# Capped attention and a spatial gating layer on one core: head pairs in twos, tails merged, and a list scheduler in the source

## The chip, the cores and the metric

One core of one Trainium2 chip runs the whole program. The metric is device time in microseconds (us) of one execution; the number for the kernel before is the median of 3 runs. The engines have short names in the profile: PE is TensorE's matmul pipe (PEld its weight loads), DVE is VectorE, ACT is ScalarE, POOL is GpSimd, SP is the engine whose queue issues all DMAs here. "L213" is line 213 of the kernel's source.

## What is computed

```python
def _attn_ref(q, k, v, cap):                 # (4, 12, 448, 64) each
    scores = np.matmul(q, k.transpose(0, 1, 3, 2)) / np.sqrt(64)
    scores = cap * np.tanh(scores / cap)
    attn = np.exp(scores - np.max(scores, axis=-1, keepdims=True))
    attn = attn / (np.sum(attn, axis=-1, keepdims=True) + 1e-09)
    return np.matmul(attn, v)

def _moe_ref(x, w_in, g_ln, w_sg, b_sg, w_out):   # x (4, 448, 768)
    h = gelu_tanh(x @ w_in)                       # w_in (768, 1024)
    u, v = h[..., :512], h[..., 512:]
    v_n = (v - mean(v)) / sqrt(var(v) + 1e-06) * g_ln
    v_s = np.einsum('ts,bsd->btd', w_sg, v_n) + b_sg[None, :, None]
    return x + (u * v_s) @ w_out                  # w_out (512, 768)
```

x is the attention output with the 12 heads side by side. w_in and w_out arrive as 64-bit words and are decoded to 32-bit floats on the chip.

## The kernel before, in words

**Attention.** The 12 heads of a batch are 6 pairs; a pair's two heads lie on the two halves of the 128 partitions. The 448 keys are cut into three chunks of 128 and a tail of 64, so a pair is 4 units and the program has 96 units (the loop over `g`). For a unit of 128 keys, `scores` makes the scores of both heads (three passes, since q and k are each split into a rounded part and a rest, `hl`; 6 matmuls, L213). For the tail, both heads' 64 keys are put side by side in `kt`, a zero-padded tile that ACT fills by two small copies for each pair (L173), and three full matmuls follow (L199); the first pair's tail is made from the unsplit data (L205). `soft` and `soft2` are tanh (L226) and exp (L229) on ACT: 128x896 for a chunk, 128x448 for a tail. `av` multiplies by the values into `pav` (L242, two matmuls for a unit, one for each head); ACT moves a finished `pav` out (L250). The softmax sums go to `den` by matmuls with a matrix of ones (L261), two units at a time. In batches 1 to 3 DVE first adds the pair's chunks and its tail to one tile (`presum`, L298: two adds of 128x896 and two of 64x448 for each pair). `recip` turns the sums of a batch into reciprocals (L318 to L323).

**The gating layer** of a batch: `norm` scales the six pairs by a matmul of the reciprocals with a selector (L335) and splits the result (L339 to L346); `hv` is the half of w_in that is normalised (four tiles, L373), `hu` the other half (four, L417), `vsg` the product with w_sg (four, L431), `outp` that with w_out (six, L460). Each product is three passes, each with its own weight load. gelu and the normalisation run on ACT and DVE.

**Weights.** `decode` takes 36 chunks of w_in and w_out, 128x256 each: a DMA into one of three pieces of `xu`, or into a free `raw` tile; the low bits (L565 on DVE for the first chunks, L568 on ACT later); L570, L572 and L575 on DVE; an add on POOL (L578); a rounding cast on DVE (L156) or ACT (L158); a subtraction on POOL (L584). The four pieces of w_sg are split by ACT and POOL (L550, L551).

**What orders the work.** The loop over `g` writes the attention in a fixed pattern. Between two units `filler` draws matmuls of the gating layer from a generator, 11 a unit (`RATE`) or 24 while a batch ends (`RATE_OUT`); `wstep` paces the decoding by the unit's number. Work that must lag is put off by `later` and `tick`. The framework then places instructions by program order and the priorities given with `tc.high_priority()`. Every engine runs its own list in order. PSUM: two double banks for scores, one bank for `pav`, one for `den`, two for the gating layer (`ps_g`).

Of the kernel before, what the change touches and what calls it, by code (L numbers as in the profile page):

```python
# [54 lines left out]
def kernel(  # L55
# [4 lines left out]
    vp: bass.AP,  # L60
    cap: bass.AP,
# [18 lines left out]
    NPAIR = B * NP  # L80
    NSTEP = NPAIR * NC
    SPB = NP * NC

    wp = ctx.enter_context(tc.tile_pool(name="wp", bufs=1))
    qk_p = ctx.enter_context(tc.tile_pool(name="qk", bufs=2))
    v_p = ctx.enter_context(tc.tile_pool(name="v", bufs=2))
    sm_p = ctx.enter_context(tc.tile_pool(name="sm", bufs=3))
    raw_s = Slots(wp, NRAW, [128, 2 * S], FP32, "raw")
    xu = wp.tile([128, 2 * NP, S], FP32, name="xu")
    xu_free = list(range(2 * NP))  # L90
    r_s = Slots(wp, 19, [128, 512], FP32R, "r")
    u_s = Slots(wp, 4, [128, S], FP32, "u")
    t_s = Slots(wp, 3, [128, 512], FP32, "t")
    ps_s = ctx.enter_context(tc.tile_pool(name="ps_s", bufs=2, space=PSUM))
    ps_a = ctx.enter_context(tc.tile_pool(name="ps_a", bufs=1, space=PSUM))
    ps_d = ctx.enter_context(tc.tile_pool(name="ps_d", bufs=1, space=PSUM))
    ps_g = ctx.enter_context(tc.tile_pool(name="ps_g", bufs=2, space=PSUM))

    win = [wp.tile([128, KD, DFF], FP32R, name=f"win{s}") for s in range(2)]
    wout = [wp.tile([128, KF, DM], FP32R, name=f"wout{s}") for s in range(2)]  # L100
    wsg = [wp.tile([128, NC, S], FP32R, name=f"wsg{s}") for s in range(2)]
    sel_r = wp.tile([128, NP, 128], FP32R, name="sel_r")
    rds = wp.tile([128, S], FP32R, name="rds")
    ones_sb = wp.tile([128, 3, NP + 31], FP32, name="ones_sb")
# [6 lines left out]
    kt = wp.tile([128, 2, 2 * TL], FP32R, name="kt")  # L111
# [4 lines left out]
    dq = []  # L116
    now = [0]

    def later(d, fn):
        dq.append((now[0] + d, len(dq), fn))  # L120

    def tick():
        now[0] += 1
        while True:
            due = [e for e in dq if e[0] <= now[0]]
            if not due:
                return
            for e in due:
                dq.remove(e)
            for e in due:  # L130
                e[2]()

    def two(t):
        return t.rearrange("p (a s) -> p a s", a=2)

    raws, qks, vs = {}, {}, {}

    def load_pair(P):
        if P >= NPAIR:
            return  # L140
        b, p = divmod(P, NP)
        raws[P] = raw_s.get()
        for i, src in enumerate((q2, k2)):
            nc.sync.dma_start(out=two(raws[P])[:, i], in_=src[b, p])

    def load_v(P):
        if P >= NPAIR:
            return
        b, p = divmod(P, NP)
        t = v_p.tile([128, S + TL], FP32, tag="v", name="v")  # L150
        nc.sync.dma_start(out=t, in_=vp[b, p])
# [8 lines left out]
    def prep_a(P):  # L160
        if P >= NPAIR:
            return
        qks[P] = qk_p.tile([128, 2, 2, S], FP32R, tag="hl", name="hl")
        cast(P // NP in DVE_Q, qks[P][:, 0], two(raws[P]))

    def prep_b(P):
        if P >= NPAIR:
            return
        hl = qks[P]
        nc.vector.tensor_tensor(out=hl[:, 1], in0=two(raws[P]), in1=f32(hl[:, 0]), op=ALU.subtract)  # L170
        for h in range(2):
            rows = slice(64 * h, 64 * h + 64)
            nc.scalar.activation(  # L173
                out=kt[rows, :, TL * h:TL * h + TL], in_=f32(hl)[rows, :, 1, 128 * FC:], func=ACTF.Copy)
        raw_s.put(raws.pop(P))

    def prep_first():
        r = two(raws[0])
        hl = qk_p.tile([128, 2, 2, S], FP32R, tag="hl", name="hl")
        for i in range(2):  # L180
            nc.vector.tensor_copy(out=hl[:, 0, i], in_=r[:, i])
            nc.vector.tensor_tensor(out=hl[:, 1, i], in0=r[:, i], in1=f32(hl[:, 0, i]), op=ALU.subtract)
        qks[0] = hl
        raw_s.put(raws.pop(0))

    sc_t, p_t, s_t, pav_t, xu_t = {}, {}, {}, {}, {}
    den_t, units_in = {}, {}

    def unit(g):
        P, c = divmod(g, NC)  # L190
        return P, c if P == 0 or c > 1 else 1 - c

# [594 lines left out]
```

## Time and profile before

| | |
|---|---|
| time, median of 3 runs | 455.83 us (455.79 to 456.27) |
| the profiled execution | 453.91 us, of which the span of its trace is 452.1 |
| busy in the span | PE 423.3 us (94%), DVE 311.6 (69%), ACT 292.2 (65%), POOL 81.7 (18%) |
| mean granted clock of TensorE | 0.985 of full speed |
| moved from and to HBM | 34.2 MB, 76 GB/s on the mean |

A busy PE is not a PE at its peak: the record of a matmul covers also the time in which it stands behind another one. The time of a stage is therefore read from the starts of the rows in it, and what an engine does in a stage from the view of stretches.

### The profile page before, as it was taken

To read this page: it belongs to the slowest core of one execution; us is meant where nothing else is said; L and a number is where in the kernel's file an instruction comes from. 1 tells how busy PE (TensorE), PEld (TensorE's weight loads), DVE (VectorE), ACT (ScalarE), POOL (GpSimd) and SP (SyncE) were. 2 spreads that over 40 slices of the span, in tenths; PEclk is the share of its full clock that TensorE was granted. 3 is DMA by queue.
4 is the path that set the end of the run, shared out by engine and by line. 5 is a ranking of instruction groups with operands and counts; after the bars stand their busy time and mean duration, and the time that the engine had idled before them with its cause. 6 is when DMAs were issued, how large, how long until landed. Compare 5 with 4: busy or idle time off the path is not lost.

```text
span 452.1 us, 5786 instructions
## 1 busy us (share of the span) xinstructions
PE 423.3 (94%) x2097; PEld 269.7 (60%) x2097; DVE 311.6 (69%) x549; ACT 292.2 (65%) x466; POOL 81.7 (18%) x97
## 2 busy tenths in 40 slices
PE   5998798996999499999999999999999999899996
PEld 2333233562665367756666667666666666579985
DVE  4945637899999764796766654877675563868652
ACT  3899899958767874486787775476778640224410
POOL 0525553266257240000000000000000000000000
PEclk9999989999999799999999999999999999999999
DMA  7673234222424223211202103210101001100012
GB/s 244 220 242 135 91 120 152 70 76 81 134 62 124 85 65 104 83 65 43 63 23 65 41 25 104 82 66 25 40 24 25 0 1 61 61 1 1 1 41 81
DMA packets 20716, 34.21 MB, mean 76 GB/s; under 512 B 3024, under 2 KB 12880, under 8 KB 20688
## 3 DMA queue, kind: packets, MB, share of 16 engines
q1 hardware_dynamic: 20688, 33.85, 23.3%
q8 instruction: 16, 0.26, 0.3%
q14 instruction: 12, 0.10, 0.1%
HBM read 28.34 MB, written 5.51 MB: 75 GB/s over the span
## 4 chain that ended last, share of the span: by engine, by line
PE 73%; DVE 12%; DMA 6%; ACT 5%; POOL 2%; issue 1%; SPq 0%; DVEq 0%; ACTq 0%
PE gp L417 14%; PE gp L460 14%; PE pav L242 12%; PE gp L373 12%; PE sc L213 8%; PE gp L431 8%; DMA xu<-in_w_in_dram 4%; PE sc L199 2%; PE den L261 2%; DVE xu L575 2%; ACT raw L226 2%; DVE raw L298 2%; PE gp L335 1%; ACT raw L229 1%; POOL xu L578 1%
## 5 line engine op out<-in xcount | busy, mean ns | idle before, releaser
L226 ACT ACTIVATE raw<-sc,qsc 128x896 f32<-128x896 f32 (+1 forms) x96 | 86.8, 909 | 39.1 <-PE sc L199 21.4
L229 ACT ACTIVATE raw<-raw,cap_sb 128x896 f32<-128x896 f32 (+1 forms) x96 | 90.0, 943 | 0.7
L242 PE MATMUL pav<-raw,v 128*64 128x448 f32 x384 | 88.8, 565 | 1.6 <-ACT xu L250 1.6
L213 PE MATMUL sc<-hl 64*128 64x448 f32 x432 | 67.5, 413 | 7.7 <-ACT raw L226 7.7
L373 PE MATMUL gp<-win,r 128*128 128x512 f32 x264 | 65.5, 398 | 2.7 <-DVE t L362 2.2
L298 DVE TENSOR_TENSOR raw<-raw,raw 64x448 f32<-64x448 f32 (+1 forms) x72 | 63.7, 885 | 5.0 <-PE pav L242 3.7
L417 PE MATMUL gp<-r,win 128*128 128x448 f32 x288 | 64.5, 372 | 0.0
L460 PE MATMUL gp<-r,wout 128*128 128x448 f32 x288 | 63.1, 371 | 0.0
L213 PEld LDWEIGHTS sc<-hl 64*128 64x128 f32 x432 | 37.4, 192 | 39.7 <-issue 15.5
L417 PEld LDWEIGHTS gp<-r,win 128*128 128x128 f32 x288 | 52.8, 188 | 13.8 <-issue 9.6
L373 PEld LDWEIGHTS gp<-win,r 128*128 128x128 f32 x264 | 48.2, 188 | 20.6 <-issue 6.1
L460 PEld LDWEIGHTS gp<-r,wout 128*128 128x128 f32 x288 | 53.1, 188 | 10.8 <-issue 3.8
L387 POOL TENSOR_TENSOR rs<-rs,pw 128x1 f32<-128x1 f32 (+1 forms) x16 | 9.9, 616 | 254.1 <-DVE rs L386 254.1
L242 PEld LDWEIGHTS pav<-raw,v 128*64 128x64 f32 x384 | 24.5, 139 | 50.6 <-issue 39.6
L431 PE MATMUL gp<-wsg,r 128*128 128x448 f32 x176 | 41.5, 382 | 4.7 <-DVE u L362 4.7
L431 PEld LDWEIGHTS gp<-wsg,r 128*128 128x128 f32 x176 | 33.0, 193 | 14.0 <-issue 5.9
L170 DVE TENSOR_TENSOR hl<-raw,hl 128x896 fp32r<-128x896 f32 x23 | 25.0, 1086 | 9.6 <-ACT hl L158 9.6
L465 DVE TENSOR_TENSOR xu<-xu,gp 128x448 f32<-128x448 f32 x24 | 14.6, 611 | 23.2 <-PE gp L460 23.0
L361 ACT ACTIVATE t<-t 128x448 f32<-128x448 f32 (+2 forms) x32 | 19.3, 602 | 15.6 <-DVE t L356 15.5
L356 DVE SCALAR_TENSOR_TENSOR t<-t,gp 128x448 f32<-128x448 f32 (+1 forms) x28 | 18.0, 644 | 15.8 <-ACT t L355 15.7
L578 POOL TENSOR_TENSOR xu<-xu 128x256 int32<-128x256 int32 x22 | 20.7, 943 | 40.6 <-DVE xu L575 40.6
L261 PE MATMUL den<-raw,ones_sb 128*32 128x448 f32 x168 | 24.6, 570 | 2.1 <-DVE raw L298 2.1
(77 smaller groups left out, 434.6 us busy)
## 6 DMA issues: line engine op xcount, KB each, us to landing
v<-in_vp_dram SPq DMA_DIRECT2D x24, 256.0 KB, 3.1
raw<-in_q_dram SPq DMA_DIRECT2D x24, 224.0 KB, 2.6
raw<-in_k_dram SPq DMA_DIRECT2D x24, 224.0 KB, 3.0
xu<-in_w_in_dram SPq DMA_DIRECT2D x21, 256.0 KB, 2.7
out_dram<-xu SPq DMA_DIRECT2D x24, 224.0 KB, 1.9
raw<-in_w_out_dram SPq DMA_DIRECT2D x11, 256.0 KB, 2.7
u<-in_w_sgT_dram SPq DMA_DIRECT2D x4, 224.0 KB, 7.2
raw<-in_w_in_dram SPq DMA_DIRECT2D x3, 256.0 KB, 2.9
```

What stands on the lines that cost most here:

```text
L170: nc.vector.tensor_tensor(out=hl[:, 1], in0=two(raws[P]), in1=f32(hl[:, 0]), op=ALU.subtract)
L213: nc.tensor.matmul(out=sc[:, h, :S], lhsT=hl[rows, w, 1, 128 * c - 128:128 * c], rhs=hl[rows, m, 0], start=(i == 0), stop=(i == 2))
L226: nc.scalar.activation(out=prob(g), in_=src, func=ACTF.Tanh, scale=qsc)
L229: nc.scalar.activation(out=prob(g), in_=prob(g), func=ACTF.Exp, scale=cap_sb)
L242: nc.tensor.matmul(out=pav_t[P][64 * h:64 * h + 64, :S], lhsT=w, rhs=two(p_t[g])[:, h if c else 0, :], start=(g % NC == 0), stop=(c == NC ...
L261: nc.tensor.matmul(out=t[32 * j:32 * j + 32, :S], lhsT=ones_sb[:, 0 if c else 1 + h, NP - 1 - P % NP:NP + 31 - P % NP], rhs=two(src)[:, h ...
L298: eng.tensor_tensor(out=a, in0=a, in1=w, op=ALU.add)
L373: yield 1, lambda i=i, c=c, a=a, w=w: nc.tensor.matmul(out=ps, lhsT=a[c][:, t * 128:t * 128 + 128], rhs=win[w][:, c, HF:], start=(i == 0), ...
L417: yield 1, lambda a=a, w=w, c=c, st=st, sp=sp: nc.tensor.matmul(out=ps, lhsT=win[w][:, c, f * 128:(f + 1) * 128], rhs=a[c][:, :S], start=s ...
L431: yield 1, lambda i=i, c=c, a=a, w=w: nc.tensor.matmul(out=ps, lhsT=a[c][:, f * 128:(f + 1) * 128], rhs=wsg[w][:, c, :], start=(i == 0), s ...
L460: yield 1, lambda ps=ps, c=c, a=a, w=w, f=f, st=st, sp=sp: nc.tensor.matmul(out=ps, lhsT=wout[w][:, f, c * 128:(c + 1) * 128], rhs=a[f][:, ...
L578: nc.gpsimd.tensor_tensor(out=a, in0=a, in1=hi_w, op=ALU.add)
```

## The change

Three things change together.

1. **Two head pairs make a group of seven units** instead of eight: three chunks of the first pair, one unit that holds the 64-key tails of both pairs, three chunks of the second. The merged tail's scores are four matmuls of 64x64 on the four quarters of the array, straight from the unsplit data (L537), for both pairs; its tanh and exp are 128x896; its values are four matmuls on the quarters (L558), with a tile `vt` of its own DMA. `kt`, its two copies for each pair, and the tail's adds on DVE are gone; the tail goes to `den` as a unit of its own, so a batch of 1 to 3 has 9 units of sums instead of 6.
2. **A list scheduler, `Plan`, is in the source.** Every operation is entered with its engine, an assumed cost, a key, a mode of the array (S scores, A values, D sums, Q quarters, G the rest) and the tiles it reads and writes. `run` repeatedly takes, over all engines, the operation that can start first; of those that can start within 0.04 us of each other on an engine the smallest key goes first, and on PE an operation of another mode has 3.92 added to its key. The order that comes out is emitted as it is (`tc.manual_schedule()`). `filler`, `wstep`, `later` and the fixed pattern are gone.
3. **Tiles and engines.** The three decoding pieces (`xb`) are the only ones, and become room for attention outputs one after the other when 12, 1 and 0 chunks are still to be placed. Four `raw` tiles hold q and k, seven `p` tiles the probabilities. `pav` and the gating layer share three PSUM banks (the gating layer at most two; norm's are not limited); at the end the scores' banks join them. The low bits of the first 12 chunks (4 in the trace of before) and 25 of the 36 casts (10) are on DVE, and so is batch 0's move of `pav` (it was ACT's). The load of `cap` is the first DMA.

```diff
-            for h in range(2):
-                rows = slice(64 * h, 64 * h + 64)
-                nc.tensor.matmul(
-                    out=sc[rows, 0, :S], lhsT=r[rows, 1, 128 * FC:], rhs=r[rows, 0],
-                    start=True, stop=True, skip_group_check=True)
...
-            add(b, 3, [(two(s_t[P])[TL * h:TL * h + TL, h, :], pr) for h, pr in enumerate(heads(small, 0))])
...
-        n = RATE_OUT if boost[0] else RATE
...
+RAWS, PS, RS, US, TS = 4, 7, 19, 4, 3
+G_CAP = 2
+DVE_CAST = (0, 1)
+DVE_EVAC = (0,)
+LOW_DVE = 12
+HI_DVE = 25
+SUMS = (False, True, True, True)
...
+class Plan:
...
+    def run(self):
...
+                first = min(x[0] for x in ests) + 0.04
+                pick = min(
+                    (x for x in ests if x[0] <= first),
+                    key=lambda x: (x[1].key + (SWITCH if e == "pe" and x[1].mode != mode else 0.0), x[1].num))
+                if best is None or pick[0] < best[0]:
+                    best = pick
...
+    sc_p = Pool([pp.tile([128, 2, 512], FP32, name=f"sc{i}") for i in range(2)])
+    ps_p = Pool([pp.tile([128, 512], FP32, name=f"ps{i}") for i in range(3)], {"g": G_CAP})
+    den_p = Pool([pp.tile([128, 512], FP32, name="den")])
...
+        def freed(b):
+            if len(st_p.queues[None]) <= (12, 1, 0)[order.index(id(b.t))]:
+                i = order.index(id(b.t))
+                for s in range(2):
+                    x_p.add(b.end, xb[i][:, s])
+                return True
+            return False
...
+        low = "dve" if j < LOW_DVE else "act"
...
+        big = "dve" if j < HI_DVE else "act"
...
+                def tail():
+                    for s in range(2):
+                        for h in range(2):
+                            rows = slice(64 * h, 64 * h + 64)
+                            nc.tensor.matmul(
+                                out=sc.t[64 * s:64 * s + 64, h, :S], lhsT=raw[s].t[rows, 1, 128 * FC:],
+                                rhs=raw[s].t[rows, 0], start=True, stop=True, skip_group_check=True)
...
+                def tail():
+                    for s in range(2):
+                        rows = slice(64 * s, 64 * s + 64)
+                        for h in range(2):
+                            nc.tensor.matmul(
+                                out=pav[s].t[64 * h:64 * h + 64, :S], lhsT=vtail.t[rows, 64 * h:64 * h + 64],
+                                rhs=p.t[rows, h, :], start=(s == 1), stop=(s == 0), skip_group_check=True)
...
+            units = [(0, c) for c in range(1, FC + 1)] + [(0, 0)] + [(1, c) for c in range(1, FC + 1)]
...
+                if not SUMS[b]:
+                    den_unit(pairs[s], 0 if c else 1, p, akey(i) + DEN, last)
+                elif c == 0:
+                    den_unit(pairs[0], 1, p, akey(i) + DEN)
...
+    with tc.manual_schedule():
+        plan.run()
```

How the instructions stand, at three places. First PE at the start of batch 0; before (`sc` scores, `pav` values, `den` sums, `raw` the probabilities, `xN` how many in a row):

```order
L205 MATMUL sc<-raw_67 64x448 x2
L213 MATMUL sc<-hl 128x448 x18
L242 MATMUL pav<-raw_69,v 64x448 x2
L242 MATMUL pav<-raw_70,v 64x448
L213 MATMUL sc<-hl 128x448 x6
L242 MATMUL pav<-raw_70,v 64x448
L199 MATMUL sc<-hl,kt 128x448 x3
L261 MATMUL den<-raw_69,ones_sb 32x448 x2
```

and with the change, where `ps` are the three shared banks, `p` the probabilities, and L537 and L558 the quarters:

```order
L529 MATMUL sc_133<-hl_89 128x448 x6
L529 MATMUL sc_134<-hl_89 128x448 x6
L529 MATMUL sc_133<-hl_89 128x448 x6
L537 MATMUL sc_134<-raw_85 64x448 x2
L537 MATMUL sc_134<-raw_86 64x448 x2
L548 MATMUL ps_135<-p_96,v_91 64x448 x2
L548 MATMUL ps_135<-p_97,v_91 64x448 x2
L529 MATMUL sc_133<-hl_90 128x448 x6
L529 MATMUL sc_134<-hl_90 128x448 x6
L548 MATMUL ps_135<-p_98,v_91 64x448 x2
L558 MATMUL ps_135<-p_99,vt_94 64x448 x2
L558 MATMUL ps_136<-p_99,vt_94 64x448 x2
```

The tail moved behind the first pair's three chunks, and operations of one kind stand together. Over the whole program the kind of work on PE changes 226 times before and 175 times with the change.

Second, DVE where batch 0's attention ends and its reciprocals are made; before (L298 adds for batch 1, L570 to L575 decoding, L339 norm):

```order
L170 TENSOR_TENSOR hl<-raw_68,hl 128x896
L572 TENSOR_SCALAR raw_72<-raw_72 128x256
L319 SCALAR_TENSOR_TENSOR t_102<-t_102,guard,den 64x448
L298 TENSOR_TENSOR raw_77<-raw_77,raw_67 64x448
L321 RECIPROCAL t_102<-t_102 64x448
L298 TENSOR_TENSOR raw_77<-raw_77,raw_67 64x448
L322 CAST rds<-t_102 64x448
L570 TENSOR_SCALAR xu<-xu 128x256
L323 TENSOR_TENSOR rds<-t_102,rds 64x448
```

and with the change (L388 to L403 and the casts to `win_61` are the decoding, COPY is the move of a finished `pav`):

```order
L312 COPY xa_80<-ps_136 128x448
L312 CAST win_61<-xb_82 128x256
L620 SCALAR_TENSOR_TENSOR t_126<-t_126,guard,den 64x448
L623 RECIPROCAL t_126<-t_126 64x448
L312 COPY xa_81<-ps_137 128x448
L388 TENSOR_SCALAR xb_83<-xb_83 128x256
L394 TENSOR_SCALAR xb_83<-xb_83 128x256
L403 SCALAR_TENSOR_TENSOR xb_83<-xb_83 128x256
L398 TENSOR_SCALAR xb_83<-xb_83 128x256
L624 CAST rds<-t_126 64x448
```

Ahead of the reciprocal 12 chunks were cast to `win` before and 6 are now; the other 30 now stand behind it, between the work of the gating layer.

Third, PE in batch 0's gating layer, where `hu` (L741) goes over to `vsg` (L758); with the change (before, one unit of scores or two of values stood between 11 matmuls of `gp` each time):

```order
L558 MATMUL ps_137<-p_99,vt_94 64x448 x2
L558 MATMUL ps_136<-p_99,vt_94 64x448 x2
L548 MATMUL ps_136<-p_101,v_91 64x448 x2
L548 MATMUL ps_136<-p_102,v_91 64x448 x2
L741 MATMUL ps_135<-r_113,win_61 128x448
L741 MATMUL ps_135<-r_114,win_61 128x448
L741 MATMUL ps_135<-r_113,win_62 128x448
L529 MATMUL sc_133<-hl_89 128x448 x6
L529 MATMUL sc_134<-hl_89 128x448 x6
L548 MATMUL ps_136<-p_98,v_91 64x448 x2
L472 MATMUL den<-p_99,ones_sb 32x448 x2
L472 MATMUL den<-p_101,ones_sb 32x448 x2
```

Two of the three shared banks (136 and 137) are values' here at the same time, and the gating layer has the third, 135; all four tiles of this batch's `vsg` follow in that one bank.

## Rows read from the trace of the kernel before

**Rows 1.** Stretches: start:end, length, busy (xcount) by engine, PEclk, DMA share, GB/s

```profile
0.00:76.70 76.70, 64.41 (x359) 25.44 (x360) 45.11 (x99) 63.91 (x102) 33.30 (x40) 0.98 0.54 175
76.70:200.20 123.50, 112.62 (x537) 70.51 (x537) 103.59 (x181) 88.56 (x155) 41.89 (x45) 0.96 0.29 88
200.20:448.50 248.30, 246.28 (x1206) 173.71 (x1204) 162.26 (x271) 139.68 (x211) 6.56 (x12) 1.00 0.12 39
100.00:140.00 40.00, 35.64 (x174) 22.19 (x173) 38.84 (x73) 30.59 (x56) 21.01 (x23) 1.00 0.30 89
```

**Rows 2.** Chain that ended last: start, length, what

```profile
21.85 4.85 DMA xu<-in_w_in_dram
...
50.79 2.62 DMA xu<-in_w_in_dram
...
76.75 2.86 DVE t L321
...
200.21 2.94 PE gp L373 x12
```

**Rows 3.** ACT's first instruction, from its groups in 0:76.7: xcount, busy, mean ns, idle before

```profile
L226 ACT ACT_TABLE_LOAD x1 | 1.3, 1283 | 6.8 <-DVE guard L661 6.8
```

**Rows 4.** Timeline of ACT, batch 0: start, length, instructions

```profile
11.78 1.91 ACT L226 ACTIVATE raw<-sc,qsc 128x896 f32<-128x896 f32 x2
13.58 1.97 ACT L229 ACTIVATE raw<-raw,cap_sb 128x896 f32<-128x896 f32 x2
```

**Rows 5.** Timeline of PE: start, length, instructions

```profile
3.97 1.76 PE L205 MATMUL sc<-raw 64*64 64x448 f32 x4 [3.97 <-DMA raw<-in_k_dram]
...
30.80 1.48 PE L213 MATMUL sc<-hl 64*128 64x448 f32 x12
...
230.30 2.49 PE L417 MATMUL gp<-r,win 128*128 128x448 f32 x11
232.72 0.88 PE L213 MATMUL sc<-hl 64*128 64x448 f32 x6
233.53 2.50 PE L417 MATMUL gp<-r,win 128*128 128x448 f32 x11
...
236.77 1.72 PE L242 MATMUL pav<-raw,v 128*64 128x448 f32 x8
238.43 2.50 PE L417 MATMUL gp<-r,win 128*128 128x448 f32 x11
...
252.03 0.96 PE L261 MATMUL den<-raw,ones_sb 128*32 128x448 f32 x8
```

**Rows 6.** Timeline of PE, the last stretch

```profile
396.10 13.89 PE L373 MATMUL gp<-win,r 128*128 128x512 f32 x60 [0.33 <-DVE r L344]
409.82 14.76 PE L417 MATMUL gp<-r,win 128*128 128x448 f32 x72
424.42 9.08 PE L431 MATMUL gp<-wsg,r 128*128 128x448 f32 x44
```

**Rows 7.** DVE's groups of the whole span: xcount, busy, mean ns, idle before

```profile
L298 DVE TENSOR_TENSOR raw<-raw,raw 128x896 f32<-128x896 f32 x36 | 39.6, 1101 | 0.6
L298 DVE TENSOR_TENSOR raw<-raw,raw 64x448 f32<-64x448 f32 x36 | 24.1, 668 | 4.5 <-PE pav L242 3.7
L575 DVE SCALAR_TENSOR_TENSOR xu<-xu 128x256 int32<-128x256 int32 x22 | 13.7, 622 | 0.2
...
L572 DVE TENSOR_SCALAR xu<-xu 128x256 int32<-128x256 int32 x22 | 8.6, 392 | 0.5
...
L156 DVE CAST win<-xu 128x256 fp32r<-128x256 f32 x10 | 2.9, 288 | 3.8 <-POOL xu L578 3.8
...
L565 DVE TENSOR_SCALAR xu<-xu 128x256 int32<-128x256 uint32 x4 | 2.2, 554 | 0.1
```

**Rows 8.** Timeline of DVE: one operation in two lengths

```profile
15.70 0.28 DVE L570 TENSOR_SCALAR xu<-xu 128x256 f32<-128x256 f32 x1
...
18.89 0.84 DVE L570 TENSOR_SCALAR xu<-xu 128x256 f32<-128x256 f32 x1
```

More of the change, by code (lines that the diff above doesn't have):

```diff
@@ L1 @@
+from collections import deque
 from contextlib import ExitStack
@@ new lines, with __init__, add, can @@
+class Pool:
+    def __init__(self, tiles, caps=None):
+        self.free = [(0.0, i, t) for i, t in enumerate(tiles)]
+        self.n = len(tiles)
+        self.queues = {}
+        self.caps = caps or {}
+        self.held = {}
+    def add(self, when, t):
+        self.free.append((when, self.n, t))
+        self.n += 1
+    def can(self, bufs):
+        by = {}
+        for b in bufs:
+            k = by.get(b.cls, 0)
+            q = self.queues[b.cls]
+            if len(q) <= k or q[k] is not b:
+                return None
+            by[b.cls] = k + 1
+            if self.held.get(b.cls, 0) + k + 1 > self.caps.get(b.cls, 99):
+                return None
+        if len(self.free) < len(bufs):
+            return None
+        return sorted(self.free)[len(bufs) - 1][0]
+    def take(self, b):
+        e = min(self.free)
+        self.free.remove(e)
+        self.queues[b.cls].popleft()
+        self.held[b.cls] = self.held.get(b.cls, 0) + 1
+        b.t = e[2]
+    def give(self, b):
+        self.held[b.cls] -= 1
+        if b.on_free is None or not b.on_free(b):
+            self.add(b.end, b.t)
@@ L177, in prep_first @@
[L177 to L191, printed above, removed]
@@ L253, in den @@
-    def den(b, units):
-        if b not in den_t:
-            den_t[b] = ps_d.tile([128, 512], FP32, tag="den", name="den")
-            units_in[b] = 0
-        t = den_t[b]
-        for half, (P, c, src) in enumerate(units):
-            for h in range(2):
-                j = 2 * half + h
-                nc.tensor.matmul(
-                    out=t[32 * j:32 * j + 32, :S],
-                    lhsT=ones_sb[:, 0 if c else 1 + h, NP - 1 - P % NP:NP + 31 - P % NP],
-                    rhs=two(src)[:, h if c else 0, :],
-                    start=(units_in[b] < 2), stop=(units_in[b] >= NP * (NC - ADDS[b]) - 2),
-                    skip_group_check=True)
-            units_in[b] += 1
@@ L710, with c_copy, mms @@
-    tail[0] = 1
-    half[0] = False
-    while flushes:
-        flush()
-    while not fill_done[0]:
-        filler(0)
-        tick()
-    while dq:
-        tick()
-_INS = ["q2", "k2", "vp", "cap", "w_in", "g_ln", "w_sgT", "b_sg", "w_out", "ones", "sel"]
+    def c_copy(eng, n, psum=False):
+        if eng == "dve":
+            return c_tt(n) if psum else c_ts(n)
+        return c_act(n, psum)
+    def mms(n, cols=None):
+        return n * ((cols or S) / 2400.0 + 0.012)
+    k_cap, k_ones, k_bsg, k_g, k_sel, k_pw, k_rds = (Buf() for _ in range(7))
@@ L724 @@
+    weights()
+    for b in range(B):
+        attention(b)
+        if b:
+            gated(b - 1)
+    gated(B - 1)
+    with tc.manual_schedule():
+        plan.run()
+_INS = ["q2", "k2", "vp", "vt", "cap", "w_in", "g_ln", "w_sgT", "b_sg", "w_out", "ones", "sel"]
 def kernel(**inputs):
@@ L750 @@
         w_sgT[:128 * FC].reshape(FC, 128, S).transpose(1, 0, 2), _np.concatenate([tail, tail])[:, None]], axis=1)
[L751 removed]
+    ones = _np.zeros((128, 2, NP + 31), _np.float32)
     ones[:, 0, NP - 1::NP] = 1.0
[L753 to L754 removed]
+    for s in range(2):
+        ones[TL * s:TL * s + TL, 1, NP - 2 + s::NP] = 1.0
     sel = _np.zeros((2, 2, 32, NP, 2, D), _np.float32)
```

1107 lines of the change are left out of this document (554 added, 553 removed).

## Prediction

> **What bounds the kernel now.** I read the stretches first, cut at two events of the chain that ended last: the reciprocal of batch 0 at 76.75, and at 200.21 the first matmul of batch 1's gating layer [rows 2]. That gives three stages [rows 1]. In stage A (0 to 76.7, batch 0's attention) ACT is busy 63.9 us of the 69.9 that are left after its first instruction waited 6.8 for `cap` [rows 3]: ACT is the bound. In stage B (76.7 to 200.2, 123.5 us, batch 0's gating layer beside attention) PE is busy 112.6 and DVE 103.6, and in its densest part DVE is busy 38.84 of 40 us [rows 1]: there DVE is the bound, with the weights' decoding between everything else. In stage C (200.2 to 448.5) PE is busy 246.3 of 248.3. Behind it 3.6 us remain for the last add and its DMA, to the span's 452.1.
>
> A busy PE can be busy badly, so I took prices from starts [rows 5, 6]. Gating matmuls: 72 take 14.60 us (409.82 to 424.42), 0.203 each, and 60 of `hv` take 13.72 (396.10 to 409.82), 0.229 each; with the program's 264 of `hv` and 776 others that makes 217.8. Twelve score matmuls take 1.48 and six 0.88, so a unit is 0.60. Among other kinds a unit takes 0.81 (232.72 to 233.53): entering scores costs 0.21. Eleven gating matmuls take 2.42 (230.30 to 232.72), 2.23 without the entry: 0.19 for entering these. Two units of values take 1.66 (236.77 to 238.43), and four sums together 0.96 less the overlap of 0.07, 0.89; if a unit of values and four sums cost the same, that is 0.77, and 0.12 for entering either.
>
> **The change on PE.** Counted in both orders with these prices. Before: 72 units of scores 43.2, 96 of values 73.9, 21 issues of sums 16.2, 23 tails of three full matmuls 14.0 and the first one 0.8; entries 75 to scores, 73 to the gating layer, 78 to others, 39.0; the gating layer 217.8. Sum 404.9. With the change: scores 43.2; 72 units of values 55.4; 24 sets of quarters, 12 for scores and 12 for values; 26 issues of sums, 20.0 (five more, since the tails are no longer added on DVE and four issues are half empty, taken at full price); entries 41, 49 and 85, 28.1.
>
> The price of four quarters has no row before. The first tail runs two quarters on the diagonal, four records, two for each matmul, in a row 1.76 us long [rows 5], in the program's first moments. Four column strips run side by side in 0.77, two row halves do so in every unit of scores. I take 0.77 for four quarters, 18.5 for all; the other bound is that two rows of quarters follow one another, 37.0; less than nothing off 0.77 has no row for it. Sum 383.0: 21.9 us less work for PE, of which 10.9 are entries.
>
> The Trainium skill (TensorE: Matmul & The Clock Gate, Part 3, Measured speedup vs the span model) has a table in which four tiles side by side give 3.07 times, not four. By that, 24 sets would cost 5.6 us more, an estimate from that page; the row of the four strips shows no such loss.
>
> **Stage A.** ACT's list up to the last exp of batch 0 holds 21 units. Two tanh take 1.80 from start to start, and two exp 1.97 less the same overlap of 0.11 [rows 4], so a unit takes 1.83, 38.4 in all. The table load and guard 1.5 [rows 3], and four copies of w_sg and one of the sums, half as wide, at some 0.54 each, make 42.6. Gone from ACT here are the copies to `kt`, the move of `pav`, low bits and casts of weights. If ACT never waits, it is through at 6.8 + 42.6 = 49.4. `cap` is now the first DMA, which could take some 2 us off the 6.8; I leave that out, since q and k must be split before the first scores. ACT was busy 91% of its part of stage A (63.9 of 69.9); at that, 42.6 take 46.6, and the reciprocal starts at **53.4**. PE's work up to the last sums is 39.8, hidden under it. DMA is busy 54% in stage A [rows 1], and the bytes fall a little (v without its padding), so I cost the 12 new loads of `vt` at nothing. SP's own list runs in order, and loads of chunks wait in it for pieces to come free; that wait is covered as long as stage B has the decoding hidden, which is the rival below. So the price of stage A is 23 us won, bounds 49.4 and 60 (ACT idle for 20%).
>
> **Stage B.** Part of that is paid back at once: of the 36 chunks 30 are now decoded behind the reciprocal, 19 before. DVE's list from the reciprocal to the first split tile of batch 1, against the same stretch before: 11 more chunks at L575's 0.62 and two operations like L572's 0.39, +15.4; 19 casts, +5.5; 6 low bits, +3.3; one more split and cast of a pair and a move of `pav`, +2; one tile of output less, -0.6; 12 adds of 128x896 for 14, and the 14 tail adds gone, -2.2 and -9.4 [rows 7]. Together +14, so 117.6 where it was 103.6. PE's work between the same points is 104.5 (144.3 less 39.8), and ACT had 88.6 here and loses the copies to `kt`, so DVE is the bound. At the 97% of its densest part that is **121 us**; bounds: 110, if PE bounds after all, and 135. The first `hv` of batch 1 then starts at 174.4, 25.8 earlier than before.
>
> **Stage C.** Before, 243.2 us of work took 248.3. With the change 238.7 remain (383.0 less the 144.3 ahead of that point); with the same 2.1% on top **243.7**. DVE had 162.3 us here and ACT 139.7 [rows 1], and both lose work; neither is near. The three shared banks cost nothing as long as attention stands between two tiles of one bank, and where it doesn't (the third place of the order: `vsg` in bank 135 alone), one such refill waits for a DVE operation, under 1 us. Bounds 239 and 251.
>
> **Sum.** 53.4 + 121 + 243.7 + 3.6 = 421.7 of span; the profiled execution has 1.8 outside its span, 423.5; the median stands 0.42% above that execution (455.83 to 453.91): **425 us**, 30.5 less. Its own range is 415 to 437.
>
> **Rivals.**
>
> *The decoding sets the pace.* For: only three pieces turn over chunks, two once 12 are left, without the free `raw` tiles of before; in the chain, four turns of the pieces take 28.9 us (first and last of five loads, 21.85 and 50.79) [rows 2], 7.2 each. At that pace 18 chunks of w_in on three pieces take 43 us, and 12 of w_out on two pieces another 43: 53.4 + 86 = 139, about when PE wants them. If queues stretch a turn to 10 us, the last comes at 53.4 + 60 + 60 = 173, with the last output tiles and the next batch's start still behind it: stage B takes some 140 us, 425 + 19 = **444**. DVE and POOL also stand in each other's way: the same L570 takes 0.28 and 0.84 [rows 8], and 23 more DVE operations on chunks (8 low bits, 15 casts) at 0.56 would add 13, 438. Of this the Trainium skill (SBUF — State Buffer, Who interferes with whom) says that the port which the two share is locked for a whole instruction. The two lengths agree with that. Against it: my prices for stage B are means that already hold such waits.
>
> *Quarters run one row after another:* 18.5 more on PE, two thirds of it where PE is the bound: **438**. Against it stand the scores' row halves.
>
> *Stage B is bound by PE:* DVE's list is shorter than my means make it, 110 for 121, and ACT starts early: **412**.
>
> *The shared banks starve PE: slower.* Two of three banks hold values for a group at a time. A gelu chain is four operations on ACT and DVE before its bank is free, 2.5 us if each takes the 0.62 of L575, the nearest row here; with one bank alone each of a batch's eight such tiles waits that long, and sixteen others for one operation: 30 us for a batch, 90 for the three that run beside attention. From a third of that uncovered it decides: the 30.5 are gone, **456** and more. Against it: in the order only a handful of refills follow their own bank directly.
>
> *It doesn't do what it says:* costs in `Plan` only set an order, and if that order stalls each engine a little everywhere, 7% over all stages, the time is the same.
>
> **Chances.** Forecast 0.62, PE-bound stage B or better 0.12, decoding 0.12, quarters 0.07, the same 0.02, starving banks and stalls beyond 0.05. The range takes in quarters and decoding: 411 to 445. What a measurement of this kernel can tell from no change is about 0.2%; faster 0.93, same 0.02, slower 0.05.
>
> **What would show it.** The first reciprocal near 53 and ACT over 85% busy ahead of it; the first `hv` of batch 1 near 174, with DVE over 93% busy in between; four quarters starting 0.77 to 0.9 before the next kind; stage C at 244 with PE never waiting over 1 us for a bank; PE's granted clock below 1.00 only in stages A and B. The prediction is wrong if the reciprocal comes late because PE or the splits (two `hl` tiles) stall batch 0, if POOL's or SP's list holds chunks back, or if PE's list, fixed against assumed costs, waits in stage C for ACT or DVE.

## The result: 435.8 us for 456.0, and the profile after

The changed kernel takes 435.8 us (median of 4 runs), before takes 456.0 beside it: ratio 0.955, 95% interval 0.953 to 0.957, faster by 4.5%. Forecast were 425 (411 to 445), so the direction and the range held and the likeliest time was 11 us too low. The profiled execution of that comparison was the one of the four that took 1306.51 us (last section); what is shown as "after" is a second trace of the same kernel, e1_same: 435.58 us, ratio 0.9559 (0.9514 to 0.9604), span 433.6.

The busy times by stretch, cut where the prediction cut (the first reciprocal of batch 0, the first `hv` of batch 1) and once more at the first `hu` of batch 0:

```profile
core 0: us, PE busy (x) PEld busy (x) DVE busy (x) ACT busy (x) POOL busy (x), PEclk, DMA share, GB/s
0.00:52.20 52.20, 45.25 (x312) 18.02 (x312) 33.52 (x64) 42.74 (x49) 15.18 (x20) 1.00 0.61 196
52.20:107.30 55.10, 41.40 (x211) 23.58 (x207) 52.85 (x117) 35.92 (x51) 27.82 (x31) 0.93 0.35 113
107.30:188.35 81.05, 73.74 (x369) 48.19 (x370) 61.67 (x115) 48.86 (x82) 32.28 (x34) 0.94 0.31 94
188.35:430.00 241.65, 240.94 (x1258) 170.51 (x1257) 151.46 (x249) 133.96 (x188) 6.57 (x12) 1.00 0.11 38
```

Against [rows 1]: stage A is 24.5 us shorter and ACT is still busy 42.74 of it, stage C 6.5 shorter and PE busy all through. Stage B got 12.5 longer (136.0 for 123.5), where a shortening of 2.5 was forecast. It has two parts of different kind: up to the first `hu` DVE is busy 52.85 of 55.1 us and PE only 41.4; behind it DVE has 19 us to spare and PE is busy 91%, part of it at the lower clock level. The events that cut it, from the timelines of DVE and PE (start, duration):

```profile
52.19 2.94 DVE L623 RECIPROCAL t<-t 64x448 f32<-64x448 f32 x1
```
```profile
107.29 6.67 PE L741 MATMUL ps<-r,win 128*128 128x448 f32 x18 [1.67 <-ACT r L314]
```
```profile
188.18 2.25 PE L694 MATMUL ps<-win,r 128*128 128x512 f32 x9
```

The 18 matmuls at 107.29 take 0.371 us each, where 0.203 is the price at 2.4 GHz [rows 6]. PE was busy for only 2.27 of the 5.29 us ahead of them (102.00 to 107.29), and the granted clock of their first 2.7 us is 0.50, the level of 1.2 GHz:

```profile
107.30:110.00 2.70, 2.70 (x7) 2.44 (x8) 2.60 (x8) 1.11 (x3) 2.37 (x2) 0.50 0.27 97
```

Four quarters, from PE's timeline:

```profile
24.43 0.98 PE L537 MATMUL sc<-raw 64*64 64x448 f32 x8
25.35 0.88 PE L529 MATMUL sc<-hl 64*128 64x448 f32 x6
...
92.23 0.98 PE L537 MATMUL sc<-raw 64*64 64x448 f32 x8
93.03 0.93 PE L558 MATMUL ps<-p,vt 64*64 64x448 f32 x8
93.89 2.48 PE L548 MATMUL ps<-p,v 128*64 128x448 f32 x12
```

A set takes 0.92 from start to start with a change of kind, 0.80 ahead of other quarters and 0.86 ahead of values.

### The profile page after: what moved, and what is told of

Read it like the earlier page. It is cut to its first block, busy times and chain, and to the rows that moved or that the text cites. A ratio compares the mean times of both kernels' runs of the same rounds, so it can differ in the third digit from the quotient of the medians.

```text
span 1304.7 us, 5767 instructions
## 1 busy us (share of the span) xinstructions
PE 1291.6 (99%) x2144; PEld 544.0 (42%) x2144; DVE 298.9 (23%) x542; ACT 266.7 (20%) x367; POOL 76.6 (6%) x96
## 4 chain that ended last, share of the span: by engine, by line
PE 99%; DVE 0%; ACT 0%; DMA 0%; issue 0%; ACTq 0%
PE ps L548 15%; PE ps L694 14%; PE ps L741 14%; PE sc L529 12%; PE ps L780 12%; PE ps L758 7%; PE den L472 6%; PE sc L780 4%; PE sc L537 3%; PE ps L558 3%; PE sc L758 2%; PE sc L694 2%; PE sc L741 2%; PE ps L651 1%; PE sc L548 1%; DMA cap_sb<-in_cap_dram 0%
## 5 line engine op out<-in xcount | busy, mean ns | idle before, releaser
L548 PE MATMUL ps<-p,v 128*64 128x448 f32 x276 | 199.4, 1649 | 0.0
L694 PE MATMUL ps<-win,r 128*128 128x512 f32 x228 | 191.9, 1086 | 0.1
L741 PE MATMUL ps<-r,win 128*128 128x448 f32 x252 | 184.0, 987 | 1.7 <-ACT xb L314 1.4
L529 PE MATMUL sc<-hl 64*128 64x448 f32 x432 | 163.4, 958 | 6.3 <-DVE hl L312 6.3
L780 PE MATMUL ps<-r,wout 128*128 128x448 f32 x216 | 160.6, 985 | 0.0
L591 ACT ACTIVATE p<-sc,qsc 128x896 f32<-128x896 f32 x84 | 84.4, 1006 | 306.7 <-PE sc L529 217.8
L741 PEld LDWEIGHTS ps<-r,win 128*128 128x128 f32 x252 | 103.5, 416 | 92.6 <-issue 86.7
L694 PEld LDWEIGHTS ps<-win,r 128*128 128x128 f32 x228 | 93.7, 415 | 99.3 <-issue 90.6
L780 PEld LDWEIGHTS ps<-r,wout 128*128 128x128 f32 x216 | 87.5, 411 | 82.4 <-issue 78.5
L758 PE MATMUL ps<-wsg,r 128*128 128x448 f32 x132 | 97.3, 977 | 0.8 <-DVE t L764 0.8
L758 PEld LDWEIGHTS ps<-wsg,r 128*128 128x128 f32 x132 | 52.9, 409 | 52.7 <-issue 49.3
```

The costliest lines, as they stand in the source:

```text
L529: nc.tensor.matmul(out=sc.t[:, h, :S], lhsT=hl[s].t[rows, w, 1, 128 * c - 128:128 * c], rhs=hl[s].t[rows, m, 0], start=(k == 0), stop=(k = ...
L548: nc.tensor.matmul(out=pav[s].t[64 * h:64 * h + 64, :S], lhsT=v[s].t[:, 128 * (c - 1) + 64 * h:128 * (c - 1) + 64 * h + 64], rhs=p.t[:, h, ...
L591: op("act", c_act(2 * S, True, True), lambda p=p, sc=sc: nc.scalar.activation(out=p.t, in_=sc.t[:, :, :S], func=ACTF.Tanh, scale=qsc), rd= ...
L694: nc.tensor.matmul(out=ps.t[:, :HF], lhsT=(xl if a else xh)[c].t[:, t * 128:t * 128 + 128], rhs=win[w][:, c, HF:], start=(c == 0 and k == ...
L741: nc.tensor.matmul(out=ps.t[:, :S], lhsT=win[w][:, c, f * 128:(f + 1) * 128], rhs=(xl if a else xh)[c].t[:, :S], start=(c == 0 and k == 0) ...
L758: nc.tensor.matmul(out=ps.t[:, :S], lhsT=(vl if a else vh)[c].t[:, f * 128:(f + 1) * 128], rhs=wsg[w][:, c, :], start=(c == 0 and k == 0), ...
```

## Experiments

The stages of every kernel, cut at the first reciprocal, the first `hv` of batch 1 and the end of PE's last matmul (us; before and after on top). "B up to `hu`" is the part of stage B ahead of the first `hu`:

| run | stage A | stage B | B up to `hu` | stage C | span | ratio to before |
|---|---|---|---|---|---|---|
| before | 76.7 | 123.5 | 40.5 | 248.4 | 452.1 | 1 |
| e1_same | 52.2 | 136.0 | 55.1 | 241.9 | 433.6 | 0.9559 |
| e2_switch0 | 52.6 | 153.5 | 56.1 | 249.4 | 459.1 | 1.0128 |
| e3_quads2 | 53.1 | 137.6 | 54.5 | 245.7 | 439.9 | 0.9687 |
| e4_pairtails | 57.0 | 148.9 | 55.3 | 242.6 | 452.2 | 0.9947 |
| e5_two_ops_out | 51.6 | 134.3 | 44.7 | 241.3 | 430.7 | 0.9486 |
| e6_no_whole | 51.5 | 132.5 | 54.6 | 239.5 | 427.1 | 0.9373 |
| e7_pieces2 | 51.9 | 161.6 | 63.7 | 241.3 | 458.3 | 1.0087 |
| e8_casts_act | 52.6 | 142.2 | 51.9 | 241.3 | 439.7 | 0.9700 |
| e9_x_parked | 52.1 | 146.4 | 57.7 | 236.0 | 438.2 | 0.9618 |
| e10_x_parked_3 | 52.7 | 132.8 | 55.5 | 240.7 | 429.8 | 0.9515 |
| e11_one_op_less | 51.3 | 141.9 | 51.0 | 241.3 | 438.1 | 0.9625 |
| e12_one_op_less_parked_3 | 51.9 | 127.7 | 49.5 | 241.3 | 424.5 | 0.9325 |

**The same kernel, the scheduler's entry cost, the quarters, the merged tails.** e1_same is the changed kernel again.

> The changed kernel once more, for a trace of an execution like the timed ones (435.8 us). The 11 us above the forecast of 425 must stand in one of three places. If quarters run one row after another, a set of four takes 1.5 us and not 0.77, and stages A and B are as forecast. If the decoding sets the pace, the first reciprocal is near 53 and the first hv of batch 1 near 185. If the fixed order stalls PE late, that hv is near 174 and stage C takes 255 us instead of 244.

The reciprocal at 52.19 and the `hv` at 188.18 are the second of these three places.

e2_switch0:

```diff
-SWITCH = 3.92
+SWITCH = 0.0
```

> SWITCH is 0: the scheduler no longer prefers work of the kind that PE is doing. PE changes its kind 256 times instead of 175. If each entry costs what the trace of before says (0.12 to 0.21 us), PE has 14.3 us more to do and the time rises by 10 to 14 us, to 446 to 450. If the entries are covered by something else (weight loads, or PE waiting for ACT and DVE anyway), it rises by less than 3.

461.29 us, 25.7 more, where the entries alone make 14.3 and 446 to 450 was expected. Counted in the two traces, 53 of the 81 entries more lie in stage C, 9.6 us by the prices, and it got 7.5 longer; 21 lie in stage B, 3.8 us by the prices, and it got 17.5 longer, at a mean clock of 0.88. So the price of an entry roughly holds where PE is the bound. What made stage B so much longer isn't shown; the order of all lists changed with this edit.

e3_quads2 issues each set of score quarters twice:

```diff
-                    for s in range(2):
+                    for s in (0, 1, 0, 1):
```

> Each set of four score quarters is issued twice (the second one overwrites the first with the same values): 12 sets more. If four quarters run side by side, 0.77 us each, at most 9 us more on PE, 7 of them outside batch 0: 442 to 445. If the two rows of quarters follow one another, 1.5 us each: 14 to 18 more, 450 to 454.

441.52 us, 5.9 more for 12 sets.

```profile
24.83 1.73 PE L537 MATMUL sc<-raw 64*64 64x448 f32 x16
26.50 0.86 PE L529 MATMUL sc<-hl 64*128 64x448 f32 x6
```

Two sets in a row start at 24.83 and the next kind at 26.50: 1.67, which is twice 0.77 and an entry of 0.12. The quarters run side by side. e4, below, shows it once more: there a set has two quarters, and it takes 0.90 to the next kind, where four take 0.92:

```profile
25.10 0.97 PE L536 MATMUL sc<-raw 64*64 64x448 f32 x4
26.00 0.96 PE L472 MATMUL den<-p,ones_sb 128*32 128x448 f32 x8
```

e4_pairtails keeps the scheduler and the new tiles and engines, and gives each pair a tail of its own (two of the four quarters, tanh and exp of half the width, the tails added to the sums by DVE again):

```diff
-            units = [(0, c) for c in range(1, FC + 1)] + [(0, 0)] + [(1, c) for c in range(1, FC + 1)]
+            units = [(s, c) for s in range(2) for c in (1, 2, 3, 0)]
...
-                    op("pe", mms(4), tail, rd=raw, wr=[sc], key=akey(i), mode="Q")
+                    op("pe", mms(4), tail, rd=[raw[s]], wr=[sc], key=akey(i), mode="Q")
```

> Only the scheduler, without the merged tails: each pair has its own tail unit again (two quarters for scores, 128x448 for tanh and exp, zero-padded values on two column strips, two adds on DVE in batches 1 to 3). By the prices PE has 398.6 us to do instead of 383.0, DVE 22 us more and ACT 5.6 more. If PE and in stage B DVE set the time, it rises by 15 to 22 us, to 451 to 458, so that nearly the whole gain is the merged tails'. If the gain is the scheduler's earlier end of batch 0, it rises by less than 8.

454.26 us, ratio 0.9947 (0.9916 to 0.9978). The change without the merged tails (the scheduler, the tiles and the engines together) wins 20 us in stage A and 6 in stage C and gives back 25 in stage B. The merged tails win 12.9 of their 18.6 us of span in stage B: with them the stage has 12 us less for DVE (126.3 busy in e4's, 114.5 in after's).

**What paces stage B.** Four kernels, each touching one thing of the decoding. e5_two_ops_out takes two of DVE's operations on a chunk away (`shift`, `sign`), e6_no_whole one of POOL's (`whole`). e7 (which also hands over the x tiles of the piece left out) and e8 are

```diff
-    st_p = Pool([t.rearrange("p a s -> p (a s)") for t in xb])
+    st_p = Pool([t.rearrange("p a s -> p (a s)") for t in xb[1:]])
...
```
```diff
-HI_DVE = 25
+HI_DVE = 12
```

> Leaves out two of the DVE operations that decode each chunk, the shift and the sign (so the weights are wrong): 36 of each, 30 of them behind the first reciprocal, where they took 339 and 497 ns, 25 us of DVE; about 20 of the 30 lie ahead of the first `hu`. In the trace of the changed kernel DVE is busy 52.85 of the 55.1 us between the first reciprocal (52.19) and the first `hu` (107.29), while PE is busy 41.4 there; after it PE is busy 73.7 of 81. Theory 1, the stage is bound by DVE up to the first `hu` and by PE behind it: 17 us come off the first part, of which PE's 13.7 us of idle time bound what can be won, first `hu` at 93 to 97, time 421 to 427. Theory 2, the order of PE's list against the assumed costs stalls it wherever DVE stands: within 3 us of 435.6. Theory 3, the pieces' turn (DMA, POOL, DVE one after another) sets the pace: a turn gets 0.8 us shorter of some 7, 5 us off, 430.

> Leaves out one of the two POOL operations of each chunk, the add of the two halves (so the weights are wrong); no DVE operation goes. 30 of them behind the first reciprocal, some 27 us of POOL. If POOL's work makes DVE's operations long (the same decoding operation takes 0.28 us in some rows and 0.82 to 0.84 in others), the means of DVE's operations between 52 and 107 fall, L394 from 0.403 to below 0.33 and the adds of 128x896 from 1.24 towards 1.08, 4 to 8 us of DVE, and the time falls to 428 to 432. If DVE's lengths have nothing to do with POOL, the means stay and only the latency of a chunk gets 0.9 us shorter: 433 to 436. If the pieces' turn sets the pace: 0.9 of some 7 us off each turn, 429 with unchanged means of DVE.

> Decodes with two pieces instead of three up to the 24th chunk; the third one's two x tiles are handed to attention at the same point of the list as before. If the turn of the pieces sets the pace (the rival of the prediction, 7.2 us a turn), 18 chunks on two pieces take 65 us for 43, the first `hu` comes some 20 us later: 450 to 456. If DVE's time sets it, the pieces only have to be ahead of DVE: 436 to 440, the few us from fewer loads in flight and from 9 more changes of kind on PE (1.5 us by the prices).

> The casts of the chunks 12 to 24 move from DVE (0.37 us) to ACT (0.44): 4.8 us less for DVE, 5.7 more for ACT in the stretch between the first reciprocal and the first `hu`, where DVE is busy 96% and ACT 65%. DVE as the bound there: 2 to 4 us won, 431.5 to 433.5. PE's list or the pieces as the bound: no change, 435 to 437. ACT's tanh and exp hurt by it more than DVE is helped: 437 to 440.

DVE as the only bound fell. Two runs take work from DVE. e5's first `hu` came 11 us earlier (96.29 for 107.29), as expected of it, and the stage became only 1.7 us shorter; its time, 432.62, lies at the edge of what the second theory allowed. e8's first `hu` came 2.8 us earlier (104.54), and the stage became 6.2 us longer; its 442.59 lies above everything that was expected of it. So DVE's time does set the first part of the stage, and what it wins there is lost behind the first `hu`.

e6, which takes nothing from DVE, won 8 us. Of the 6.5 us that its span is shorter, 3.5 are in stage B and 2.4 in stage C, where POOL has next to nothing to do. DVE's operations between 52 and 107, first after, then e6:

```profile
L403 DVE SCALAR_TENSOR_TENSOR xb<-xb 128x256 int32<-128x256 int32 x14 | 7.8, 559 | 0.4
L394 DVE TENSOR_SCALAR xb<-xb 128x256 f32<-128x256 f32 x14 | 5.2, 372 | 0.0
L610 DVE TENSOR_TENSOR p<-p,p 128x896 f32<-128x896 f32 x4 | 4.9, 1230 | 0.0
```
```profile
L403 DVE SCALAR_TENSOR_TENSOR xb<-xb 128x256 int32<-128x256 int32 x17 | 8.0, 468 | 2.5 <-ACT xb L390 1.9
L394 DVE TENSOR_SCALAR xb<-xb 128x256 f32<-128x256 f32 x17 | 5.9, 346 | 0.0
L605 DVE TENSOR_TENSOR p<-p,p 128x896 f32<-128x896 f32 x4 | 4.3, 1068 | 0.0
```

The means fell, though L394's not to the 330 ns of the first theory, and 17 chunks passed where 14 had. So signs of contention and of a shorter turn came together, and this run doesn't part them.

e7 lost 24.5 us (450 to 456 was expected if the pieces' turn sets the pace, 460.1 measured). The way wasn't the expected one: the first `hu` came 8 us later and not 20 (115.62 for 107.29), and 17 us were lost behind it.

The pieces are also batch 1's x tiles. In after's trace, rows of POOL, then ACT, then PE:

```profile
113.70 1.11 POOL L418 TENSOR_TENSOR win<-xb,win 128x256 fp32r<-128x256 f32 x1 [0.22 <-DVE win L312]
```
```profile
114.81 0.97 ACT L314 ACTIVATE xb<-ps 128x448 f32<-128x448 f32 x2
```
```profile
115.40 3.31 PE L741 MATMUL ps<-r,win 128*128 128x448 f32 x15 [1.45 <-ACT xb L314]
```

The values of batch 1's first group were done on PE at 96.37 (93.89 + 2.48, above) and lay in two of the three shared banks until 114.81, when POOL was through with that piece (113.70 + 1.11). That is the piece of the 22nd chunk, the first one that is given up. On two pieces the move came at 146.32.

**The two limits apart and together.** e9_x_parked stores batch 0's x to its place in the output and reads it back for the last add, so that batch 1's x needs no piece; e10 also keeps three pieces to the end of w_out. e11 fuses two of DVE's operations into one; e12 is e10 and e11 together.

```diff
+            if b == 0:
+                op("sp", 0.065, lambda p=p: nc.sync.dma_start(out=outT[b, p], in_=xr[p].t), ...
...
+            if b == 0:
+                x = Buf(u_p)
+                op("sp", 0.065, lambda: nc.sync.dma_start(out=x.t, in_=outT[b, c]), ...
```
```diff
-            if len(st_p.queues[None]) <= (12, 1, 0)[order.index(id(b.t))]:
+            if len(st_p.queues[None]) <= (2, 1, 0)[order.index(id(b.t))]:
```
```diff
-            nc.vector.tensor_scalar(out=a, in0=f32(hi), scalar1=2.0 ** -112, scalar2=None, op0=ALU.mult)
...
-                out=a, in0=a, scalar1=3, scalar2=0x7FFFFFF8, op0=ALU.logical_shift_left, op1=ALU.bitwise_and)
+                out=a.bitcast(I32), in0=hi, scalar1=3, scalar2=0x3FFFFFF8,
+                op0=ALU.logical_shift_left, op1=ALU.bitwise_and)
```

> Batch 0's six normalised x tiles are written to their place in the output and read back into `u` tiles for the last add (12 more DMAs of 229 KB, no other work), so that batch 1's x takes batch 0's tiles at about 75 us and not the halves of the decoding pieces. Theory, the decoding sets the pace through these tiles: in the traces so far the values of batch 1's first group are moved to x within 2 us of the last chunk of w_in (114.8 with 113.7 to 120.5 in the changed kernel, 146.3 with 146.9 on two pieces, 125.4 with 124.9 with casts on ACT), holding two of three banks until then. With the tiles free earlier that move comes before 105, PE's 21 us of idle time behind the first reciprocal halve, and the time is 423 to 430. Rival, the chunks themselves (PE waiting for weights) set the pace: the move comes earlier and the time stays within 2 us of 435.6. Rival, DVE bounds up to the first `hu` and PE's list stalls behind it: within 3 us; the DMAs' cost with nothing won: 436 to 440.

> As the one before, and since no x waits for a piece any more, all three pieces decode w_out to its last two chunks, where one was given up after w_in. If the turn of the pieces still paces w_out once x no longer hangs on it (PE's matmuls with `wout` from about 160 on), 2 to 5 us below the one before; if only x hung on it, within 2 us of the one before, or a little above for 5 more changes of kind on PE (0.8 us by the prices).

> Two of DVE's operations on each chunk become one: the shift by three with a mask that also clears the second highest bit does what the scaling by 2^-112 and the shift did, for weights below 2 in magnitude. 36 operations of 0.40 us less for DVE, 30 of them behind the first reciprocal, 12 us; nothing else changes but the order that follows from it. What the runs so far leave standing is that two things limit the stretch from the first reciprocal to about 165 us in turn: DVE's time (busy 95% up to the first `hu`) and the pieces, which are the x tiles of batch 1. With DVE alone relieved the first `hu` comes earlier, at 98 to 102 for 107.3, and the pieces hold the values of batch 1's first group until the last chunk of w_in all the same: 430 to 434. If DVE's time were all, 424 to 426.

> The same fused operation, and with it batch 0's x parked in the output, and three pieces to the end of w_out: both limits relieved at once. Alone, parking gave 0.9 us of 435.6 and one limit less on DVE (two operations left out) 3.0. If the two limits stand one behind the other, together they give more than their sum: first `hu` at 98 to 102, batch 1's first hv before 180, 420 to 427. If they are independent small things, 430 to 433. If something else paces the stretch (PE's list stalling by its order), no better than the better of the two alone.

e9 took 439.02 us and e10 434.70 (0.9454 to 0.9576, not to be told from e1_same): the moves came at 103.6 and 102.2 and the time didn't follow, so that theory fell too, alone. e10 is 4.3 us below e9, as it should be if the turn still paces w_out. (e9's stages can't be compared one by one: 441 matmuls stand between its first `hu` and the `hv`, where after has 369.) e11 took 439.75, if anything worse than the changed kernel (0.9592 to 0.9659 against 0.9514 to 0.9604), where 430 to 434 was expected. e12 took **426.34** (0.929 to 0.936), where 420 to 427 was expected: parking together with the third piece is worth 13.4 us with the operation gone and 1 or 2 with it there. The 28 us from 102, in windows of after, e11 and e12 (columns as above):

```profile
102.00:130.00 28.00, 23.53 (x100) 17.08 (x99) 24.88 (x52) 15.69 (x28) 16.42 (x17) 0.88 0.24 68
```
```profile
102.00:130.00 28.00, 20.48 (x75) 14.22 (x73) 20.36 (x40) 12.93 (x25) 16.06 (x18) 0.77 0.21 64
```
```profile
102.00:130.00 28.00, 25.06 (x121) 16.58 (x121) 24.51 (x47) 17.54 (x30) 15.76 (x19) 0.88 0.29 88
```

In e11 the first `hu` starts 5 us earlier and then neither PE (20.48) nor DVE (20.36) is full. PE's timeline there, first e11, then e12:

```profile
102.31 5.02 PE L737 MATMUL ps<-r,win 128*128 128x448 f32 x18
112.29 6.68 PE L737 MATMUL ps<-r,win 128*128 128x448 f32 x18 [4.97 <-DVE u L678]
121.52 4.17 PE L544 MATMUL ps<-p,v 128*64 128x448 f32 x12 [2.55 <-DVE u L678]
```
```profile
101.34 6.97 PE L741 MATMUL ps<-r,win 128*128 128x448 f32 x33
108.24 2.48 PE L544 MATMUL ps<-p,v 128*64 128x448 f32 x12
110.64 0.87 PE L741 MATMUL ps<-r,win 128*128 128x448 f32 x3
```

With two banks held, e11's `hu` go through the one that is left and wait 4.97 us for its gelu; the two banks come free by the move at 120.72. In e12 the moves start at 98.71 and 102.44, and 33 matmuls run through. e5 and e8, the other two runs with less work for DVE and x in the pieces, stand the same way at the second 18 `hu`:

```profile
109.32 5.75 PE L729 MATMUL ps<-r,win 128*128 128x448 f32 x18 [4.32 <-DVE u L670]
```
```profile
118.27 5.34 PE L741 MATMUL ps<-r,win 128*128 128x448 f32 x18 [5.77 <-DVE u L682]
```

In e11 it isn't the piece itself that holds the banks so long. Rows of POOL, then ACT:

```profile
110.73 1.56 POOL L414 TENSOR_TENSOR win<-xb,win 128x256 fp32r<-128x256 f32 x1 [0.23 <-DVE sm L711]
```
```profile
119.01 0.54 ACT L671 ACTIVATE t<-ps 128x448 f32<-128x448 f32 x1 [4.32 <-PE ps L737]
120.24 0.58 ACT L676 ACTIVATE t<-t 128x448 f32<-128x448 f32 x1 [0.69 <-DVE t L673]
120.72 1.07 ACT L314 ACTIVATE xb<-ps 128x448 f32<-128x448 f32 x2
```

POOL is through with the 22nd chunk at 112.29 (110.73 + 1.56). The moves stand behind a gelu in ACT's list, that gelu waits for the second 18 `hu`, and these wait for a bank: so the moves come 8 us after their piece. With x parked `Plan` has tiles early and puts the moves ahead. No run puts them ahead and changes nothing else.

So the stage has two parts. Up to the first `hu` it follows DVE's list: e5, e8 and e11 make that part 10.4, 3.2 and 4.1 us shorter, e6 and e10, which take nothing from DVE, leave it as it was. Behind it stand 80.9 us in after, and 89.6, 90.3 and 91.0 in these three, whose `hu` start sooner but have one bank. With x parked and three pieces it is 77.3 (e10) and 78.3 (e12), and there PE is full, busy 97% and 95%; in e11 it is 84%. e6, whose pieces are through sooner, comes to 78.0 with x in them. The rows of e10, e12 and e11:

```profile
108.17:185.51 77.34, 74.96 (x394) 46.66 (x393) 68.25 (x123) 52.75 (x86) 33.83 (x37) 1.00 0.40 125
```
```profile
101.34:179.61 78.27, 74.40 (x390) 48.12 (x388) 62.66 (x112) 53.39 (x88) 34.70 (x39) 0.96 0.41 125
```
```profile
102.31:193.26 90.95, 76.28 (x376) 51.26 (x375) 60.42 (x102) 51.86 (x85) 33.13 (x36) 0.91 0.27 84
```

The pieces' turn is no shorter in e12: its last chunk of w_in is through on POOL's list no sooner than after's (the subtraction starts at 122.77 for 120.51). What got faster is what no longer waits for a piece. One rival stays: each edit lets `Plan` make another order of all lists, and no run holds the order fixed, so differences of a few us can be the order's. The loss behind the first `hu` came in three different orders.

## Why the prediction was right, and which term was mis-sized

*Stage A* was right: reciprocal at 52.19 for 53.4, ACT busy 42.74 for 42.6, which is 94% of the 45.4 us behind 6.8, for 91%. The time that was allowed for waits of ACT went elsewhere: its last exp ends at 48.92, near the 49.4 of an ACT that never waits, and 3.3 us of sums, their move and one operation of DVE stand between that and the reciprocal.

*Stage B* is the term that was off: 136.0 for 121, and it is the whole miss. DVE's work was right: 114.5 busy (52.85 + 61.67) for 117.6. (Its 11 more chunks agree with the trace of before, where 17 chunks pass L575 and 16 are cast to `win` ahead of the reciprocal; the 12 given with the order of the lists is too low.) The step that failed is "so DVE is the bound. At the 97% of its densest part that is 121 us". DVE is that full (96%) only up to the first `hu`, and 84% over the whole stage, where the sign was over 93%; behind the first `hu` it has time to spare and PE is the fuller engine. 117.6 at 97% took one bound for a stretch that has two, one behind the other. Added by parts, DVE's 52.85 and PE's 73.74 make 126.6; the other 9.4 us of the 136.0 are waits, 2.2 ahead of the first `hu` and 7.2 behind it. PE's busy time was 115.1 for 104.5. Part of that is the lower clock: means of 0.93 and 0.94 are worth at most 8.7 us here (0.07 of 55.1 and 0.06 of 81.05, an estimate). Another part is that busy time stands above the price anyway, 45.25 for 39.8 in stage A at a clock of 1.00.

*The rival on decoding* had nearly the size, but not the way. It put a stretched turn at 10 us, the last chunk of w_out at 173 and stage B at 140. Measured: the last subtraction of w_out at 174.60; 18 chunks of w_in between 51.66 and 120.51 on three pieces, a turn of 11.5, of which the load is 3.1 (median from issue to landing); 12 of w_out from there to 174.60 on two, 9.0. It doesn't reach PE through weights that come late (PE waits 1.9 us for `win` in all) but through the pieces' second use as x tiles, and with it two of three banks. Of its other half, DVE and POOL in each other's way, e6 shows that means of DVE's operations fall when POOL does less; L519's didn't (1127 to 1257 ns, three operations each). The Trainium skill (SBUF — State Buffer, Who interferes with whom) says that VectorE and GpSimd share a pair of ports that one instruction holds to its end; the means that fell agree with it.

*Stage C* was right: 241.9 for 243.7, and PE's longest wait there is 0.7 us. *The end* took 3.5 us for 3.6, and 1.8 lie outside the span; the 0.42% that were added for the median had no counterpart (435.58 to 435.43), 1.6 us. The sum closes: 425 - 1.2 + 15.0 - 1.8 - 0.1 - 1.6 = 435.3.

*Quarters*: 0.77 and an entry of 0.12 were right (e3). By the factor 3.07 that the Trainium skill gives for four row tiles (TensorE: Matmul & The Clock Gate, Part 3, Measured speedup vs the span model) a set would take 1.00, an estimate from that page; the row at 92.23 has 0.80, so for these quarters the measurement decides for less. *The shared banks* starve PE nowhere for 30 us a batch, but in stage B they are how the lateness arrives; a kernel with a smaller share of banks for the gating layer wasn't run. *It doesn't do what it says*: for the change without the merged tails this was nearly true in the sum (e4), by a large gain and a large loss.

What stays open: how much of e6's 8 us is contention and how much a shorter turn; what made stage B of e2 so long; and whether the moves alone, put ahead in ACT's list, would win what parking wins.

## What to carry to other kernels

Cut a stage wherever the engine that is full changes, and add up the maxima of the parts; one engine's mean share over the stage hides where the others starve. A tile with two uses makes the first use's pace the bound of the second: look at who gets a buffer next, not only at who fills it. In a fixed list the operation that frees a buffer can stand behind one that waits for it: look at its place in the list too. Where two limits stand one behind the other, relieving one shows nothing or a loss, and only a run with both relieved tells that from a wrong theory.

## What the hardware showed unasked

One execution of the changed kernel took 1306.51 us, three times the others, with the same instructions. Groups of PE's instructions of it (busy us, mean ns, idle before), and one of ACT's:

```profile
L548 PE MATMUL ps<-p,v 128*64 128x448 f32 x276 | 199.4, 1649 | 0.0
L780 PE MATMUL ps<-r,wout 128*128 128x448 f32 x216 | 160.6, 985 | 0.0
L591 ACT ACTIVATE p<-sc,qsc 128x896 f32<-128x896 f32 x84 | 84.4, 1006 | 306.7 <-PE sc L529 217.8
```

The same groups of e1_same have means of 553, 371 and 1006 ns. The records of all kinds of matmuls are 2.2 to 3.0 times as long, PE is busy 99% of the span, and DVE and ACT are busy about as long as ever (298.9 and 266.7 us, for 300.1 and 261.5). From start to start it is more: 11 matmuls of L758 take 8.01 us there (1233.33 to 1241.34), 0.73 each, and 2.28 in e1_same (410.64 to 412.92), 0.21 each:

```profile
1233.33 8.16 PE L758 MATMUL ps<-wsg,r 128*128 128x448 f32 x11
1241.34 8.17 PE L758 MATMUL sc<-wsg,r 128*128 128x448 f32 x11
```
```profile
410.64 2.44 PE L758 MATMUL ps<-wsg,r 128*128 128x448 f32 x11
412.92 2.43 PE L758 MATMUL sc<-wsg,r 128*128 128x448 f32 x11
```

The level of 1.2 GHz made 0.371 of 0.203 above, so it wouldn't explain a factor of 3.5. The page of this execution has no row of the granted clock, so what PE was granted isn't known, and the cause stays open.
